# Sliding-window attention beside an SSM convolution: one DRAM tensor for Z and u·D, and loads of 96 rows in place of 32

## The chip, the cores and the metric

The kernel runs on one core of one Trainium2 chip. The core has a matrix engine (PE, with a separate row PEld for its weight loads), a vector engine (DVE), a scalar engine (ACT), GpSimd (POOL) and SyncE (SP). SP and POOL issue the transfers (DMAs) here; sixteen DMA engines move the data. Every engine works through its own instructions in order, and semaphores tie the engines together. The metric is device time in microseconds; each kernel is run several times and the median is given.

## The reference

Two independent halves are computed and put side by side, each 2048 positions by 640 channels:

- *Half a*: `qkv = x @ wqkv`, 32 heads of 20; each position attends to the 8 positions `s, s-2, ..., s-14` (those before the start are masked); softmax over the 8; weighted sum of `v`; then `@ wo`.
- *Half b*: for each channel `d` a convolution of `u` with a kernel `K[d, l] = Re(sum_n C[d,n] exp(dt[d] A[d,n] l) dt[d] B[d,n])`, with 192 states `n`, done in the reference through an FFT of twice the length (`y = irfft(rfft(u) * rfft(K))[:2048]`, rounded to bf16), and then `y + u * Dskip`.

Inputs and outputs are bf16.

## The kernel before

**Channels and chunks.** The 640 channels of half b are worked on in five chunks of 128 (`NCH = 5`). For one chunk the kernel first builds the convolution kernel `K` from tables (`trig_half`, `small_half`, `y_form`, `kgen_unit`), then transforms `K` and `u` (`fwd`), multiplies the spectra (`products`) and does the first half of the inverse transform (`inverse_a`). The result is `Z`, a tile of 128 partitions by 4096: 32 frequencies times 4 channel groups on the partitions (frequency major, group minor), and along the row the real part of 64 positions times 32 channels followed by the imaginary part.

**What goes through DRAM.** Three scratch tensors carry data from the chunks to later work. `Sd` holds the spectrum of `u`: it is stored by `fwd_u` (L394) and loaded back by `products` as `P1` (L353) and, with its halves exchanged, as `P2` (L354, L355); the two products with the spectrum of `K` are L357. `Zd` holds `Z`, stored by `inverse_a` (L376) as soon as its fourth piece is done. `UDd` holds `u * Dskip`: `times_d` multiplies half a chunk at a time on DVE (L386) into one buffer `UD` of 128 partitions by 1024, and SP stores it (L387), ten times in all. In `UD` the partition is group major, position minor, the other way round from `Z`.

**The end of half b.** `Inverse` finishes the inverse transform. Its 64 positions are cut into four quarters of 16; for one quarter the tile `self.t[qr]` has 96 partitions: 32 rows for the real part, 32 for the imaginary part, 32 for `u * Dskip`. The constant `HB` on the same 96 partitions holds cosines, sines and an identity, so one matmul (L676) does the second transform step and adds `u * Dskip`. `Inverse.load` fills a quarter chunk by chunk, three transfers of 32 rows for each chunk (L664), 60 transfers in all; in the first and fourth quarter they alternate between SP and POOL, in the others all are on SP. A row has four pieces (one per channel group) of 512 elements. `Inverse.part` does two or three positions: matmuls into `ps_ib`, an ACT copy into `ysb` (L677), and after every eighth position four stores of 32 partitions to the output (L680) on SP. `ysb` has four such groups, used in turn.

**The order of the work.** The chunks' loop in `body` issues the stages of half b, then attention starts: projections of `k`, `q` and `v`, products of `q` and `k` on DVE (L529, L532), logits on PE (L543), softmax, and the weighted sum `av_step` (products on DVE at L603, summed on PE into `ps_o`), with the output projection `out_piece` (`ps_op`, stores at L637). The parts of `Inverse` are dealt out between the steps of `av_step` by the lists `inside` and `behind`; quarter 0 and 1 are loaded before that loop, quarters 2 and 3 chunk by chunk from within it (`LOADS`). A quarter's tile takes the place of an older tile: quarter 1 that of `kT` (last read by the products of L532), quarter 2 that of `prod`, quarter 3 that of `xT` (last read by the projection of `v`), and its loads wait until these have been read.

Where a call is not marked with `keep_in_program_order`, a scheduler in the framework puts the instructions of each engine in order by its own estimates; from `att.in_order()` on, PE, ACT and the softmax keep the order written. The DMAs of SP stand in the order that this scheduler chose. Each DMA from SP counts up one of eight semaphores in turn, so that the ninth waits for the first.

Between the last `times_d` and the P1 load of chunk 3, `load_x` has SP issue four transposing loads of `x` into `xT` (L431).

Of the kernel before, what the change touches and what calls it, by code (L numbers as in the profile page):

```python
# [13 lines left out]
bf16 = mybir.dt.bfloat16  # L14
f32 = mybir.dt.float32

NCH = 5
# [64 lines left out]
def inline(nc, arr, name):  # L82
    return nc.inline_tensor(np.ascontiguousarray(arr).astype(np.float32).astype(ml_dtypes.bfloat16), name=name).ap()


def partB_prep(tc, pools, prm):
# [33 lines left out]
    for nm in ("B_B_re", "B_B_im", "B_C_re", "B_C_im"):  # L120
        load(nm)
# [144 lines left out]
def bc(ap, axis, n):  # L266
    s = list(ap.shape)
    return ap.unsqueeze(axis).to_broadcast(s[:axis] + [n] + s[axis:])
# [94 lines left out]
def inverse_a(tc, pools, C, P1, P2, Zd, pool):  # L363

    nc = tc.nc
    MM = nc.tensor.matmul
    Z = pool.tile([128, 128, 32], bf16, name="Z", tag="sp", bufs=3)

    def piece(b):
        ps = pools["psum"].tile([128, 8, 128], f32, name="ps_ia", tag="bank2")  # L370
        for j in range(8):
            for w, P in enumerate((P1, P2)):
                MM(ps[:, j], lhsT=P[:, 8 * b + j].rearrange("p k g -> p (k g)"), rhs=C["EA"][:, w, :], start=(j % 4 == 0 and w == 0), stop=(w == 1), skip_group_check=True)  # L373
        nc.scalar.copy(out=Z[:, :, 8 * b:8 * b + 8], in_=ps[:].rearrange("p j x -> p x j"))  # L374
        if b == 3:
            nc.sync.dma_start(out=Zd, in_=Z[:].rearrange("p x j -> p (x j)"))  # L376

    return [lambda b=b: piece(b) for b in range(4)]


def times_d(tc, pools, C, UDd, c, i):

    nc = tc.nc
    U = C["U"][:].rearrange("p l (ut c) -> p c l ut", c=NCH)[:, c]
    UD = pools["tabb"].tile([128, 32, 32], bf16, name="UD", tag="UD")
    tc.keep_in_program_order(nc.vector.tensor_tensor(out=UD[:], in0=U[:, 32 * i:32 * i + 32], in1=bc(C["Dsb"][:, c], 1, 32), op=A.mult))  # L386
    nc.sync.dma_start(out=UDd[c, :, 1024 * i:1024 * i + 1024], in_=UD[:].rearrange("p l j -> p (l j)"))  # L387


def fwd_u(tc, pools, C, Sd, c):  # L390
# [11 lines left out]
class Attention:  # L402
# [4 lines left out]
    def __init__(self, tc, pools, A_x, A_wqkv, A_wo, out_a, psk, psg):  # L407
        self.tc, self.nc, self.ta, self.ident = tc, tc.nc, pools["bbase"], pools["ident"]
        self.A_x, self.A_wo, self.out_a = A_x, A_wo, out_a
        self.wsrc = A_wqkv.rearrange("(kt k) c -> k kt c", k=128)  # L410
        self.big = lambda name: psk.tile([128, 2, 512], f32, name=name, tag="bank2")
        self.one = lambda name: psg.tile([128, 512], f32, name=name, tag="bank", bufs=2)
        self.lsb, self.at, self.obs = {}, {}, {}
        self.nav = self.nob = 0
        self.MM = self.nc.tensor.matmul
        self.SC = self.VV = lambda ins: ins
# [226 lines left out]
class Inverse:  # L643


    def __init__(self, att, a2, Zd, UDd, out_b):
        self.att, self.nc, self.a2, self.Zd, self.UDd = att, att.nc, a2, Zd, UDd
        self.dst = out_b.rearrange("(l1 l0) (g ch) -> g l1 l0 ch", l0=64, g=4)
        self.HB = att.ta.tile([96, 64, 32], bf16, name="HB", tag="TA1")
        self.nc.gpsimd.dma_start(out=self.HB[:].rearrange("p a n -> p (a n)"), in_=inline(self.nc, fft_consts_np()["HB"], "c_HB"))  # L650
        self.t = {}
# [4 lines left out]
    def load(self, qr, c0=0, c1=NCH):  # L656
        nc = self.nc
        pool, tag = ((self.a2, "Z"), (self.att.ta, "LPC"), (self.att.a1, "prod"), (self.att.ta, "U"))[qr]
        if c0 == 0:
            self.t[qr] = pool.tile([96, 4, NCH, 16, 32], bf16, name="Z", tag=tag)  # L660
        for c in range(c0, c1):
            for ri in range(3):
                src = self.UDd[c, :, 512 * qr:512 * qr + 512] if ri == 2 else self.Zd[c, :, 2048 * ri + 512 * qr:2048 * ri + 512 * qr + 512]
                (nc.sync, nc.gpsimd)[(c + ri) % 2 if qr in (0, 3) else 0].dma_start(out=self.t[qr][32 * ri:32 * ri + 32, :, c].rearrange("p g l n -> p g (l n)"), in_=src.rearrange("(g p) n -> p g n" if ri == 2 else "(p g) n -> p g n", g=4))  # L664

    def part(self, l0, n):
        nc = self.nc
# [15 lines left out]
        return [(lambda l0=8 * q + l, n=n: self.part(l0, n)) for q in range(8) for l, n in ((0, 3), (3, 3), (6, 2))]  # L683


def body(tc, ctx, pools, prm, B_u, B_Dskip, Sd, Zd, UDd, A_x, A_wqkv, A_wo, out_a, out_b):
    nc = tc.nc
    cn = fft_consts_np()
    bbase = ctx.enter_context(tc.tile_pool(name="taba", bufs=1, reuse_waits="tile"))
# [9 lines left out]
    C = dict(BD=BD, T2=T2, EA=EA, Dsb=Dsb, U=U)  # L699
# [25 lines left out]
    att = Attention(tc, pools, A_x, A_wqkv, A_wo, out_a, psk, psg)  # L725
# [5 lines left out]
    def unit(c, h, uu, F, G, X, between=lambda: None):  # L731
        Ys = [y_form(tc, pools, F, G, uu, k) for k in range(3)]
        between()
        kgen_unit(tc, dict(pools, psum=psg), 2 * h + uu, X, Ys, Kb[c])
        if 4 * c + 2 * h + uu in UD_AFTER:
            times_d(tc, pools, C, UDd, *divmod(UD_AFTER.index(4 * c + 2 * h + uu), 2))

    def q_first():
        att.open_first(pools["tabb"])
# [5 lines left out]
    UD_AFTER = [2, 3, 5, 6, 7, 9, 10, 11, 13, 14]  # L745
# [75 lines left out]
            att.products(1, w, ct, ct + 1)  # L821
    fft.close()
    a2 = ctx.enter_context(tc.tile_pool(name="a2", bufs=1, side="right", reuse_waits="tile"))
    inv = Inverse(att, a2, Zd, UDd, out_b)
    inv.load(0)
    att.open_v()
    for w in range(W):
# [35 lines left out]
    for i0, ni, j0, nj, done, inside, behind in (  # L863
# [7 lines left out]
        for w in range(W):  # L871
# [5 lines left out]
            if (done, w) in LOADS:  # L877
                qr, c = LOADS[done, w]
# [9 lines left out]
@with_exitstack  # L888
def kernel(
    ctx: ExitStack,  # L890
    tc: tile.TileContext,
    A_x: bass.AP,
    A_wqkv: bass.AP,
    A_wo: bass.AP,
    B_u: bass.AP,
    B_A_re: bass.AP,
    B_A_im: bass.AP,
    B_B_re: bass.AP,
    B_B_im: bass.AP,
    B_C_re: bass.AP,  # L900
    B_C_im: bass.AP,
    B_log_dt: bass.AP,
    B_Dskip: bass.AP,
    out: bass.AP,
):
    nc = tc.nc
    prm = dict(B_A_re=B_A_re, B_A_im=B_A_im, B_B_re=B_B_re, B_B_im=B_B_im, B_C_re=B_C_re, B_C_im=B_C_im, B_log_dt=B_log_dt)
    out_a = out[0][:, 0:640]
    out_b = out[0][:, 640:1280]
    pools = {}  # L910
    pools["const"] = ctx.enter_context(tc.tile_pool(name="const", bufs=1))
    idc = nc.inline_tensor(np.eye(128, dtype=np.float32).astype(ml_dtypes.bfloat16), name="ident_c")
    ident = pools["const"].tile([128, 128], bf16, name="ident")
    nc.sync.dma_start(out=ident[:], in_=idc.ap())
    pools["ident"] = ident
    dpool = ctx.enter_context(tc.tile_pool(name="dram", bufs=1, space=bass.MemoryType.DRAM))
    Sd = dpool.tile([NCH, 128, 4096], bf16, name="Sdram")
    Zd = dpool.tile([NCH, 128, 4096], bf16, name="Zdram")
    UDd = dpool.tile([NCH, 128, 2048], bf16, name="UDdram")
    body(tc, ctx, pools, prm, B_u, B_Dskip, Sd, Zd, UDd, A_x, A_wqkv, A_wo, out_a, out_b)  # L920


# [28 lines left out]
```

## Time and profile before

| | us |
|---|---|
| median of 3 runs | 422.47 (420.15 to 423.2) |
| the profiled execution | 420.89 |
| its span | 419.0 |
| busy: PE / DVE / ACT / POOL | 343.7 / 380.0 / 310.4 / 44.6 |
| SP, all issues of the 10 stores of UD | about 0.32 each |
| SP, issue of one load of 32 rows of Z | about 0.59 |

Moved in all: 51.57 MB, 123 GB/s on average; 41.40 MB of it on SP's queue. The share of busy time is an average over stages with different limits. The views that are quoted below give start and duration in microseconds; in brackets stands how long an engine had been idle before an instruction and what released it. A line such as L664 is a line of the kernel as printed above, SPq is SP's instruction queue, and "issue" in the chain of work is time in which an engine waited for nothing that the profile shows.

### The profile page before, as it was taken

To read this page: it belongs to the slowest core of one execution; us is meant where nothing else is said; L and a number is where in the kernel's file an instruction comes from. 1 tells how busy PE (TensorE), PEld (TensorE's weight loads), DVE (VectorE), ACT (ScalarE), POOL (GpSimd) and SP (SyncE) were. 2 spreads that over 40 slices of the span, in tenths; PEclk is the share of its full clock that TensorE was granted. 3 is DMA by queue.
4 is the path that set the end of the run, shared out by engine and by line. 5 is a ranking of instruction groups with operands and counts; after the bars stand their busy time and mean duration, and the time that the engine had idled before them with its cause. 6 is when DMAs were issued, how large, how long until landed. Compare 5 with 4: busy or idle time off the path is not lost.

```text
span 419.0 us, 17077 instructions
## 1 busy us (share of the span) xinstructions
PE 343.7 (82%) x7757; PEld 232.6 (56%) x7757; DVE 380.0 (91%) x353; ACT 310.4 (74%) x571; POOL 44.6 (11%) x85
## 2 busy tenths in 40 slices
PE   2476679968888787786967798999899999789896
PEld 1133575845855577554755567455455676445454
DVE  7999999799997999999999989984986999999842
ACT  3988988789899899969999682533667644745652
POOL 7520000000000000000010000040000300502110
PEclk9997889999898899989989988999999999969889
DMA  5599003261333313344029990610040382887643
GB/s 144 182 226 162 3 2 127 89 214 34 127 128 129 85 22 127 127 130 102 15 115 304 188 250 9 242 78 2 3 102 0 109 183 86 222 233 206 186 122 108
DMA packets 45129, 51.57 MB, mean 123 GB/s; under 512 B 31376, under 2 KB 38992, under 8 KB 42368
## 3 DMA queue, kind: packets, MB, share of 16 engines
q1 hardware_dynamic: 41520, 41.40, 36.2%
q0 software_dynamic: 3392, 8.95, 7.0%
q8 instruction: 61, 1.00, 1.0%
q10 hardware_dynamic: 144, 0.12, 0.1%
q14 instruction: 12, 0.10, 0.1%
HBM read 28.01 MB, written 18.35 MB: 111 GB/s over the span
## 4 chain that ended last, share of the span: by engine, by line
PE 40%; ACT 23%; DVE 21%; issue 9%; DMA 4%; SPq 3%; DVEq 0%; ACTq 0%
PE ps_k L322 8%; ACT R L223 6%; ACT A L337 6%; ACT Sg L343 5%; PE ps_q L490 4%; PE ps_k L472 4%; PE ps_v L503 4%; PE ps_op L421 4%; DVE Y L307 3%; DMA P<-Sdram 3%; DVE X L277 3%; ACT Z L374 3%; PE ps_ph L248 2%; PE ps_l L543 2%; PE ps_ph L252 2%
## 5 line engine op out<-in xcount | busy, mean ns | idle before, releaser
L307 DVE TENSOR_TENSOR Y<-F,G 128x3072 bf16<-128x3072 bf16 x60 | 103.0, 1758 | 2.5 <-PE ps_k L322 2.5
L322 PE MATMUL ps_k<-Y,X 64*32 64x64 bf16 (+1 forms) x3840 | 80.8, 237 | 17.3 <-issue 7.8
L322 PEld LDWEIGHTS <-X 64*32 64x32 bf16 (+1 forms) x3840 | 61.8, 115 | 44.3 <-issue 28.4
L223 ACT ACTIVATE R<-LPC 128x192 bf16<-128x192 f32 x225 | 59.5, 358 | 0.1
L248 PE MATMUL ps_ph<-LPC 128*128 128x512 bf16 x100 | 33.1, 434 | 11.9 <-DMA LPC<-lo 5.9
L343 ACT CAST Sg<-ps_f 128x1024 bf16<-128x1024 f32 x40 | 37.6, 1027 | 5.8 <-PE ps_f L342 5.8
L342 PE MATMUL ps_f<-A,T 128*128 128x128 bf16 x320 | 26.3, 252 | 17.2 <-ACT A L337 16.2
L337 ACT CAST A<-ps_f 128x1024 bf16<-128x1024 f32 x40 | 38.0, 1042 | 2.1 <-PE ps_f L336 2.0
L342 PEld LDWEIGHTS <-T 128*128 128x128 bf16 x320 | 24.6, 115 | 18.6 <-issue 17.6
L277 DVE TENSOR_TENSOR X<-R,TX 128x3072 bf16<-128x3072 bf16 x20 | 34.3, 1758 | 0.0
L260 ACT ACTIVATE TA<-ps_ph 128x1024 bf16<-128x1024 int16 (+1 forms) x40 | 30.5, 831 | 4.4 <-PE ps_ph L252 2.4
L603 DVE TENSOR_TENSOR prod<-v,atp 128x2048 bf16<-128x2048 bf16 (+2 forms) x32 | 30.9, 1016 | 2.2 <-PE ps_o L421 1.3
L260 ACT ACTIVATE TX<-ps_ph 128x1024 bf16<-128x1024 int16 (+1 forms) x40 | 30.0, 843 | 1.7 <-PE ps_ph L252 1.4
L532 DVE TENSOR_TENSOR prod<-qT,kT 128x1024 bf16<-128x1024 bf16 (+1 forms) x16 | 23.0, 1481 | 4.7 <-ACT qT L491 4.7
L357 DVE TENSOR_TENSOR P<-P,Sg 128x4096 bf16<-128x4096 bf16 x10 | 22.9, 2289 | 3.4 <-DMA P<-Sdram 1.7
L421 PE MATMUL ps_op<-wo,o 128*128 128x320 bf16 x160 | 25.0, 304 | 0.4 <-DVE recip L572 0.3
L373 PE MATMUL ps_ia<-EA,P 128*128 128x128 bf16 x320 | 23.2, 231 | 0.9 <-DVE P L357 0.9
L374 ACT CAST Z<-ps_ia 128x1024 bf16<-128x1024 f32 x20 | 19.5, 1014 | 5.9 <-PE ps_ia L373 4.7
L336 PE MATMUL ps_f<-BD,U 128*64 128x128 bf16 x320 | 20.2, 283 | 4.2 <-ACT Z L374 3.5
L635 ACT CAST ob<-ps_op 128x320 bf16<-128x320 f32 x28 | 11.8, 431 | 15.0 <-PE ps_op L421 12.5
L490 PE MATMUL ps_q<-xT,wkq 128*128 128x512 bf16 x100 | 22.6, 379 | 0.0
L472 PE MATMUL ps_k<-xT,wkq 128*128 128x512 bf16 x100 | 22.4, 379 | 0.0
(132 smaller groups left out, 591.1 us busy)
## 6 DMA issues: line engine op xcount, KB each, us to landing
Sdram<-Sg SPq DMA_DIRECT2D x5, 1024.0 KB
P<-Sdram SPq DMA_DIRECT2D x5, 1024.0 KB
P<-Sdram SPq DMA_DIRECT2D x10, 512.0 KB
Zdram<-Z SPq DMA_DIRECT2D x5, 1024.0 KB
Z<-Zdram SPq DMA_DIRECT2D x30, 128.0 KB
U<-in_B_u_dram SPq DMA_DIRECT2D x4, 640.0 KB
UDdram<-UD SPq DMA_DIRECT2D x10, 256.0 KB
out_dram<-ysb SPq DMA_DIRECT2D x32, 80.0 KB
```

What stands on the lines that cost most here:

```text
L223: last = nc.scalar.activation(out=R[:, :, e, :], in_=src, func=ACT.Exp, scale=m)
L248: MM(full[:, 16 * gi:16 * gi + 16], lhsT=L[b][:, 0:128], rhs=C, start=(i == 0), stop=(i == len(ops) - 1))
L260: last = nc.scalar.activation(out=dst[:, q0:q0 + nq, 0:32, :].rearrange("p q e f -> p e q f"), in_=words.rearrange("p (e q f) -> p e q f", ...
L277: TT = lambda o, a, b, op: V.tensor_tensor(out=o, in0=a, in1=b, op=op)
L307: nc.vector.tensor_tensor(out=Y[:].rearrange("p q (b a) f -> p q b a f", a=8), in0=fa, in1=gb, op=A.mult)
L322: MM(ps[32 * g:32 * g + 32, t], lhsT=X[hb, q, 2 - k, :, f], rhs=Ys[k][hb, q, :, f], start=(t == 0 and n == 0), stop=(n == 5), tile_positio ...
L337: nc.scalar.copy(out=A1[:, :, 32 * b:32 * b + 32].rearrange("p k (j g) -> p k j g", g=4), in_=ps[:].rearrange("p j k g -> p k j g"))
L342: last = MM(ps[:, kk], lhsT=C["T2"][:, 8 * b + kk, :], rhs=A1[:, 8 * b + kk, :], start=(kk % 4 == 0), stop=True, skip_group_check=True)
L343: nc.scalar.copy(out=Sg[:, :, 8 * b:8 * b + 8, :], in_=ps[:].rearrange("p k (j g) -> p j k g", g=4))
L421: self.MM = lambda *a, **k: late(self.nc.tensor.matmul(*a, **k))
L472: MM(ps[:, i], lhsT=self.wk[:, kt, 128 * ct:128 * ct + 128], rhs=self.x4[:, kt, 2 * i:2 * i + 2, 256 * hf:256 * hf + 256], start=(kt == 0) ...
L490: MM(ps[:, i], lhsT=self.wq[:, kt, 128 * ct:128 * ct + 128], rhs=self.x4[:, kt, 2 * i:2 * i + 2, 256 * hf:256 * hf + 256], start=(kt == 0) ...
```

## The change

`Zd` becomes one tensor of shape `[5, 3, 128, 2048]`: real part, imaginary part and `u * Dskip`, each 128 rows of 2048. The store of `Z` writes the two parts of a row to two places. `times_d` writes its rows in the same order as `Z` (frequency or position major, group minor); as its tile is group major, the store becomes four, one for each group of 32 partitions. With that the three parts of a quarter are evenly spaced rows, and one transfer of 96 rows by four pieces replaces three of 32; all of them are issued by SP, none by POOL.

```diff
-            nc.sync.dma_start(out=Zd, in_=Z[:].rearrange("p x j -> p (x j)"))
+            nc.sync.dma_start(out=Zd[0:2].rearrange("r p n -> p r n"), in_=Z[:].rearrange("p (r l) j -> p r (l j)", r=2))
...
-def times_d(tc, pools, C, UDd, c, i):
+def times_d(tc, pools, C, Zd, c, i):
...
-    nc.sync.dma_start(out=UDd[c, :, 1024 * i:1024 * i + 1024], in_=UD[:].rearrange("p l j -> p (l j)"))
+    dst = Zd[2].rearrange("(p g) n -> g p n", g=4)[:, :, 1024 * i:1024 * i + 1024]
+    for g in range(4):
+        nc.sync.dma_start(out=dst[g], in_=UD[32 * g:32 * g + 32].rearrange("p l j -> p (l j)"))
...
-            for ri in range(3):
-                src = self.UDd[c, :, 512 * qr:512 * qr + 512] if ri == 2 else self.Zd[c, :, 2048 * ri + 512 * qr:2048 * ri + 512 * qr + 512]
-                (nc.sync, nc.gpsimd)[(c + ri) % 2 if qr in (0, 3) else 0].dma_start(out=self.t[qr][32 * ri:32 * ri + 32, :, c].rearrange("p g l n -> p g (l n)"), in_=src.rearrange("(g p) n -> p g n" if ri == 2 else "(p g) n -> p g n", g=4))
+            src = self.Zd[c].rearrange("r (p g) n -> (r p) g n", g=4)[:, :, 512 * qr:512 * qr + 512]
+            nc.sync.dma_start(out=self.t[qr][:, :, c].rearrange("p g l n -> p g (l n)"), in_=src)
...
-            times_d(tc, pools, C, UDd, *divmod(UD_AFTER.index(4 * c + 2 * h + uu), 2))
+            k, i = divmod(UD_AFTER.index(4 * c + 2 * h + uu), 2)
+            times_d(tc, pools, C, Zd[k], k, i)
...
-    Zd = dpool.tile([NCH, 128, 4096], bf16, name="Zdram")
-    UDd = dpool.tile([NCH, 128, 2048], bf16, name="UDdram")
+    Zd = dpool.tile([NCH, 3, 128, 2048], bf16, name="Zdram")
```

More of the change, by code (lines that the diff above doesn't have):

```diff
@@ L643, with __init__ @@
 class Inverse:
-    def __init__(self, att, a2, Zd, UDd, out_b):
-        self.att, self.nc, self.a2, self.Zd, self.UDd = att, att.nc, a2, Zd, UDd
+    def __init__(self, att, a2, Zd, out_b):
+        self.att, self.nc, self.a2, self.Zd = att, att.nc, a2, Zd
         self.dst = out_b.rearrange("(l1 l0) (g ch) -> g l1 l0 ch", l0=64, g=4)
@@ L683, in parts, with body @@
         return [(lambda l0=8 * q + l, n=n: self.part(l0, n)) for q in range(8) for l, n in ((0, 3), (3, 3), (6, 2))]
-def body(tc, ctx, pools, prm, B_u, B_Dskip, Sd, Zd, UDd, A_x, A_wqkv, A_wo, out_a, out_b):
+def body(tc, ctx, pools, prm, B_u, B_Dskip, Sd, Zd, A_x, A_wqkv, A_wo, out_a, out_b):
     nc = tc.nc
@@ L823, in body @@
     a2 = ctx.enter_context(tc.tile_pool(name="a2", bufs=1, side="right", reuse_waits="tile"))
-    inv = Inverse(att, a2, Zd, UDd, out_b)
+    inv = Inverse(att, a2, Zd, out_b)
     inv.load(0)
@@ L917 @@
     Sd = dpool.tile([NCH, 128, 4096], bf16, name="Sdram")
[L918 to L920 removed]
+    Zd = dpool.tile([NCH, 3, 128, 2048], bf16, name="Zdram")
+    body(tc, ctx, pools, prm, B_u, B_Dskip, Sd, Zd, A_x, A_wqkv, A_wo, out_a, out_b)
 _INS = ['A_x', 'A_wqkv', 'A_wo', 'B_u', 'B_A_re', 'B_A_im', 'B_B_re', 'B_B_im', 'B_C_re', 'B_C_im', 'B_log_dt', 'B_Dskip']
```

## The prediction

> **What bounds the kernel now.** I read the page first. One execution spans 419.0 us (420.89 us with what lies around the span), DVE is busy for 91% of it and PE for 82%, while the row of DMA busy tenths has zeros beside nines.
>
> ```profile
> span 419.0 us, 17077 instructions
> ...
> PE 343.7 (82%) x7757; PEld 232.6 (56%) x7757; DVE 380.0 (91%) x353; ACT 310.4 (74%) x571; POOL 44.6 (11%) x85
> ...
> DMA  5599003261333313344029990610040382887643
> ```
>
> The reader is to see that no share of the whole decides anything here: the change touches DMAs alone, so it counts only where a transfer ends a wait. For that I read the chain of work that ended last (columns: start us, us, what), from its end backwards.
>
> ```profile
> 381.93 1.85 SPq L680
> 383.78 0.04 issue
> ...
> 390.30 3.12 DMA Z<-Zdram
> ...
> 393.44 0.60 PE ps_ib L421 x24
> ...
> 415.52 0.49 DVE ob L633
> ```
>
> The last 25.6 us are PE work without a gap (393.44 to the DVE cast at 415.52 and the store behind it), and ahead of them the chain runs for some twelve us through SP's queue: output stores (L680), 0.04 us between one issue and the next, then loads of Z for the third and fourth quarter (L664), and 3.12 us in which the last of them lands. The PE timeline (idle time before, and its releaser, in brackets) gives the size of that wait, and DVE's shows who else stands still.
>
> ```profile
> 366.61 0.75 PE L421 MATMUL ps_ib<-Z,HB 96*32 96x160 bf16 x24
> ...
> 391.05 0.66 PE L421 MATMUL ps_o<-prod,ident 32*32 32x256 bf16 x40
> 393.44 0.60 PE L421 MATMUL ps_ib<-Z,HB 96*32 96x160 bf16 x24 [1.74 <-DMA Z<-Zdram]
> ```
>
> ```profile
> 391.42 2.43 DVE L603 TENSOR_TENSOR prod<-v,atp 128x1024 bf16<-128x1024 bf16 x3 [0.74 <-PE ps_o L421]
> 394.41 1.23 DVE L603 TENSOR_TENSOR prod<-v,atp 128x2048 bf16<-128x2048 bf16 x1 [0.56 <-PE ps_o L421]
> ```
>
> PE sat for 1.74 us because the third quarter's tile was not there; DVE waited in that stretch for PE (0.74 and 0.56 us), not the other way round. So 1.74 us is what an earlier landing is worth here. The wait falls where it does because SP works in order, and the loads are interleaved with stores that wait for ACT. Sizes of both, from SP's timeline of the last third:
>
> ```profile
> 349.79 1.19 SPq L664 DMA_DIRECT2D Z<-Zdram  x2
> ...
> 360.06 1.23 SPq L664 DMA_DIRECT2D Z<-Zdram  x1
> 365.33 2.61 SPq L680 DMA_DIRECT2D out_dram<-ysb  x4
> ```
>
> Between the load that was issued at 360.06 and the first store at 365.33 SP only waited.
>
> There is a second place where a transfer is on the chain, 150 us earlier: the product of chunk 3's spectra (P, L357).
>
> ```profile
> 241.13 3.76 ACT Sg L343 x4
> ...
> 247.04 0.68 ACT TA L260
> 247.72 0.86 issue
> 248.59 2.29 DVE P L357
> 250.88 1.68 DVE Y L307
> ...
> 252.60 0.48 PE ps_k L322 x20
> ```
>
> Sg, which this product also reads, left ACT at 241.13 + 3.76 = 244.89. The view names ACT's TA as releaser, but L260 writes nothing that P reads, and 0.86 us of "issue" lie between the two, where a hand-over elsewhere takes 0.04 (the row at 383.78 is one). What else P needs is the load of P1 from Sdram, so I take that load to have landed at about 248.5. SP's timeline shows why it came late.
>
> ```profile
> 225.79 0.32 SPq L387 DMA_DIRECT2D UDdram<-UD  x1
> 226.21 15.30 SPq L431 DMA_TRANSPOSE xT<-in_A_x_dram  x4
> 241.61 0.52 SPq L353 DMA_DIRECT2D P<-Sdram  x1
> 243.66 0.46 SPq L354 DMA_DIRECT2D P<-Sdram  x1
> ```
>
> P1's load at 241.61 stood behind four transposing loads of x (15.30 us of issue), and these behind the UD store of 225.79. Whatever lengthens that store moves the transposes, P1's load, the product at 248.59, the Y behind it and PE's matmuls at 252.60, all on the chain.
>
> **The change part by part.** The order of instructions in the built program says what moves: the orders of PE, ACT and DVE stay as they are; POOL loses its 14 loads of Z; SP issues 20 loads of 96 rows for 46 of 32, and 40 UD stores of 32 rows for 10 of 128; and all 20 loads now stand in SP's queue ahead of all 32 output stores of ysb. Three durations are needed (min/median/max in ns of an issue on SP):
>
> ```profile
> L387 SPq DMA_DIRECT2D UDdram<-UD x10: 319/322/351, 68.8 to 225.8; - x10
> ```
>
> ```profile
> L680 SPq DMA_DIRECT2D out_dram<-ysb x32: 315/464/1849, 365.3 to 407.8; - x32
> ```
>
> ```profile
> L664 SPq DMA_DIRECT2D Z<-Zdram x30: 542/594/1478, 332.3 to 390.3; - x30
> ```
>
> 1. *The loads of the last two quarters.* SP alone, issuing a 128 KB load every 0.6 us, kept the DMA engines at a share of 0.57 and 169 GB/s; with POOL and the stores beside it the share was 0.95 at 239 GB/s (windows from 349.80 and 365.00; the last three columns are the clock granted to PE, DMA share and GB/s).
>
> ```profile
> core 0: us, PE busy (x) PEld busy (x) DVE busy (x) ACT busy (x) POOL busy (x), PEclk, DMA share, GB/s
> 349.80:362.00 12.20, 11.15 (x288) 6.61 (x281) 11.28 (x12) 6.83 (x10) 2.13 (x4) 1.00 0.57 169
> 365.00:375.00 10.00, 8.40 (x220) 4.02 (x220) 10.00 (x11) 5.93 (x12) 1.21 (x3) 0.66 0.95 239
> 395.00:410.00 15.00, 14.91 (x316) 8.04 (x316) 8.67 (x8) 9.76 (x21) 1.62 (x3) 0.80 0.49 123
> ```
>
> The ten loads of 384 KB for the last two quarters are 3.93 MB: at 169 to 239 GB/s that is 16.4 to 23.3 us from the gate at about 360.1 (xT's last reader and PE's first free moment for the third quarter), so they have landed by 377 to 384, and PE asks for the third quarter at 391.05 + 0.66 = 391.71. The wait of 1.74 us goes. What is late next? PE's own work, 14.91 of the 15 us from 395; DVE runs at PE's pace there. Bounds: 0, if the loads still come late, and 1.74; I take −1.74. The issue time of a 96-row transfer is in no row. From below it is a 32-row issue, 0.59; from above three of them, 1.8. Even at 1.8 us the ten are issued by 378.5, so both ends give −1.74. The second quarter, gated at 349.79, is five loads: 1.97 MB, 11.6 us at 169 GB/s, landed by 361.4, before the first matmul on it in the row at 366.61. Stores now queue behind the loads, but the ring of ysb holds four groups and its first slot is written again only after 391.71. At nothing, then, with PE's other work as cover; without that cover one more load time, about 3.1 us.
>
> The Trainium skill, "DMA: Bandwidth & Descriptors", section "Issuing engines are not separate DMA queues", says that issuing from several engines only saves the sequencer's time, which is usually small beside the transfer. Here the trace disagrees: at 0.57 the engines waited for SP. By the page the merged loads would gain nothing from fewer issues; the sum does not need that gain, only the place in the queue.
>
> 2. *The UD stores.* One issue of 0.32 us becomes four. Nearest row: a 32-row store of ysb, median 0.46, min 0.315, max 1.85. With 0.04 us between issues four take 4 × 0.46 + 3 × 0.04 = 1.96, so what follows on SP is 1.64 us later; 1.06 us with the minimum. At nine of the ten places something covers it: behind the second store of the two pairs stands a P1 load, as in chunk 2, where the pair below ends at 175.03 + 6.54 = 181.57 and the product that reads P1 starts sixteen us later; behind the others stand stores of Sg and Z, or nothing.
>
> ```profile
> 175.03 6.54 SPq L387 DMA_DIRECT2D UDdram<-UD  x2
> ```
>
> ```profile
> 197.28 2.30 DVE L357 TENSOR_TENSOR P<-P,Sg 128x4096 bf16<-128x4096 bf16 x1
> ```
>
> At 225.79 nothing covers it. Part may be taken back by the first transpose, which alone took longer than its sisters:
>
> ```profile
> 226.21 4.46 SPq L431 DMA_TRANSPOSE xT<-in_A_x_dram  x1
> ```
>
> 4.46 against (15.30 − 4.46) / 3 = 3.61: 0 to 0.85 us, since it shared the engines with a 1 MB store; I take 0.4. So +1.24 us (bounds 0, if P1's load was not the releaser after all, and 1.64). The second half of P2 waits until 243.66 anyway, and P1 at 242.85 is still ahead of it.
>
> 3. *One buffer for UD.* The next UD product must wait until all four pieces have landed. The tightest pair is the one above: SP issues from 175.03, DVE writes again at 179.90.
>
> ```profile
> 179.90 1.32 DVE L386 TENSOR_TENSOR UD<-U,Dsb 128x1024 bf16<-128x1024 bf16 x1
> ```
>
> Three pieces later is 175.03 + 1.5 = 176.53; a 160 KB store of the same kind lands 2.0/3.5/5.0 us after its issue:
>
> ```profile
> DMA to landing us min/median/max: 2.0/3.5/5.0
> ```
>
> That is 178.5, 180.0 or 181.5 for 179.90: 0, 0.1 or 1.6 us, and DVE is not on the chain there. I take 0.
>
> 4. *Z stored in rows of 4 KB instead of 8 KB, and POOL without loads.* The last of the five stores is read back by the first quarter's loads, which SP has issued before the second quarter's gate at 349.79 and PE wants only shortly before the row at 366.61; the earlier four have whole chunks of time. POOL has no work that waits behind its loads but the output stores. 0 for both.
>
> Sum: −1.74 + 1.24 = −0.5 us on 420.89, that is 420.4. The profiled execution stands 1.6 us below the median of the three runs (422.47; 420.15 to 423.2); on the median's footing the forecast is 422.0 us. One per cent is 4.2 us, about what a measurement of this kernel can tell from no change, so this is "same".
>
> **The rivals.**
>
> A. *Only the gain.* The transposes absorb the delay, or P1's load was not what P waited for: −1.74, 420.7. For it: the profile does name ACT as the releaser. Against: the 0.86 us without a cause.
>
> B. *The pieces hold SP for longer (slower).* With t us for each piece, SP reaches the transposes 4t − 0.2 us later, and with 0.4 taken back and 1.74 gained the net is 4t − 2.34: it turns to a loss at t = 0.59, and passes 1% at t = 1.64. At 1.85, the longest store of ysb, it is +5.1 us, 427.6. For it: issues next to a busy DMA did get that long, and the store at 225.79 meets a 1 MB store. Against: the single issue at that very spot took 0.32. The Trainium skill, "DMA: Bandwidth & Descriptors", section "Anatomy of one DMA", gives a DMA a fixed cost of about 2.0 us; paid one after another by four pieces that would be some +5.7 us by the same formula, an estimate. Loads 0.6 us apart show that here such costs overlap, so this gets a small chance.
>
> C. *Merging does not cheapen the issue.* The dearest issue of many small rows is this one:
>
> ```profile
> L720 SPq DMA_DIRECT2D U<-in_B_u_dram x4: 597/1182/2988, 23.4 to 31.9; - x4
> ```
>
> At 2.99 us each the second quarter lands at 349.8 + 15 + 3.1 = 367.9, 1.3 us late for 366.61, and the ten others at about 393.5, so that the old wait stays: 1.24 + 1.3 = +2.5, 425.0.
>
> D. *The clock.* In 395 to 410 PE was granted 0.80 and was busy throughout. Without the pause it may get full speed there, 3 us more: −3.5, 419.0. Nothing shows that the pause caused the low clock.
>
> **How the numbers follow.** The rivals' times stand on the 420.89 of the profiled execution. Forecast 0.48 (its own range 420.9 to 422.4: −1.74 + 1.06 − 0.85 to −1.74 + 1.64), A 0.18, B 0.20 (half of it past 1%), C 0.07, D 0.07. Faster by over 1% needs D and A together (−4.7): 0.05. Slower: 0.10 from B and 0.02 from C, where a late second quarter would also hold DVE. Within 1%: 0.83. The range takes in D at 419.0 with the spread of the runs, and reaches into B: 418.5 to 426.
>
> **What would show it.** In the changed profile: no wait of PE's ps_ib for Z near 391; twenty Z loads ahead of the first ysb store on SP, landed before 385; four UD issues at about 225.8 that total near 2 us, the transposes starting near 227.8, and P (L357) near 249.8 instead of 248.59, with the Y and ps_k behind it as much later. The forecast is wrong if a UD piece takes more than 0.6 us, if a 96-row issue takes more than 1.8 us, or if P stays at 248.6.

## The result: slower by 1.4%, and the profile after

The changed kernel takes 427.52 us (median of six runs, 425.62 to 429.91) against 421.34 us for the kernel before (six runs, 419.22 to 423.2): a ratio of 1.014, 95% interval 1.0093 to 1.0187. The forecast was 422.0 us, range 418.5 to 426; the time lies outside it. The profiled execution of the changed kernel took 425.62 us, its span is 423.8 us, 4.8 us more than before. Here and below a ratio goes by the executions that were not in a slower state, a median by all of them, so a ratio can differ by some half a per cent from the quotient of two medians.

From the page of the changed kernel, the head, the PE row and the DMA row of the 40 slices, and the two queues that carry instructions (packets, MB, share of 16 engines):

```profile
span 423.8 us, 17050 instructions
...
PE 336.1 (79%) x7739; PEld 227.9 (54%) x7757; DVE 380.7 (90%) x353; ACT 310.6 (73%) x571; POOL 38.9 (9%) x71
...
DMA  5599003262334403334149971700040658994153
...
q8 instruction: 60, 0.98, 1.0%
...
q14 instruction: 12, 0.10, 0.1%
```

The busy times are no higher than they were (DVE 380.7 for 380.0, PE lower); the time that was added is idle time. At 360 us the two profiles are still close together: the first exponentials of the attention start 0.3 us later. ACT's timeline, before and then after:

```profile
360.09 1.91 ACT L562 ACTIVATE lsb<-lsb 128x2048 bf16<-128x2048 bf16 x1
```

```profile
360.39 1.91 ACT L564 ACTIVATE lsb<-lsb 128x2048 bf16<-128x2048 bf16 x1
```

The loss lies between 363 and 386 us. The chain of work that ended last, after, in that stretch (start us, us, what):

```profile
363.35 0.47 PE ps_ib L423 x14
363.82 2.71 issue
366.52 0.45 PE ps_ib L423 x6
...
370.57 0.44 PE ps_o L423 x5
371.00 4.11 issue
375.12 0.85 PE ps_o L423 x23
...
380.64 0.28 PE ps_o L423 x5
380.92 0.94 issue
381.86 0.37 PE ps_o L423 x11
```

Three times PE stops and the profile shows nothing that it waits for: 2.71 + 4.11 + 0.94 = 7.76 us. Each time it stops in the middle of a group: 14 of 20 matmuls of `ps_ib`, then the pause, then the other 6; 5 of 16 of `ps_o`, then 11. The matmuls on both sides of such a pause read the same tiles. Before, there is one pause of that kind in the stretch, 0.94 us (PE's timeline, before; the later rows are for the sum below):

```profile
368.73 0.54 PE L421 MATMUL ps_o<-atp,ident 32*32 32x384 bf16 x14 [0.94 <-issue]
...
370.78 1.89 PE L421 MATMUL ps_s<-lsb,ident 128*128 128x256 bf16 x8
...
375.24 0.84 PE L421 MATMUL ps_op<-wo,o 128*128 128x320 bf16 x5 [0.30 <-DVE recip L572]
...
376.32 0.85 PE L421 MATMUL ps_op<-wo,o 128*128 128x320 bf16 x5
...
377.41 1.53 PE L421 MATMUL ps_op<-wo,o 128*128 128x320 bf16 x10
...
407.96 7.46 PE L421 MATMUL ps_op<-wo,o 128*128 128x320 bf16 x50
```

The same matmuls in PE's timeline after:

```profile
369.57 0.99 PE L423 MATMUL ps_ib<-Z,HB 96*32 96x160 bf16 x24
...
377.17 1.89 PE L423 MATMUL ps_s<-lsb,ident 128*128 128x256 bf16 x8
...
382.16 1.38 PE L423 MATMUL ps_op<-wo,o 128*128 128x320 bf16 x5
...
383.95 1.51 PE L423 MATMUL ps_op<-wo,o 128*128 128x320 bf16 x5
...
385.84 1.53 PE L423 MATMUL ps_op<-wo,o 128*128 128x320 bf16 x10
...
399.48 0.66 PE L423 MATMUL ps_o<-prod,ident 32*32 32x256 bf16 x40
400.36 0.72 PE L423 MATMUL ps_ib<-Z,HB 96*32 96x160 bf16 x24 [0.23 <-ACT ob L637]
...
413.06 7.46 PE L423 MATMUL ps_op<-wo,o 128*128 128x320 bf16 x50
```

Laid side by side, the lateness grows and then shrinks: `ps_ib` x24 366.61 to 369.57 (+2.96), `ps_s` 370.78 to 377.17 (+6.39), the first `ps_op` x10 377.41 to 385.84 (+8.43), the third quarter's `ps_ib` x24 393.44 to 400.36 (+6.92), the last `ps_op` x50 407.96 to 413.06 (+5.10). The sum of the parts:

| part | us |
|---|---|
| late from the head | +0.30 |
| pauses of PE without a releaser, 7.76 − 0.94 | +6.82 |
| the two `ps_op` x5 behind them, 1.38 + 1.51 for 0.84 + 0.85 (granted clock 0.53 for 1.00) | +1.20 |
| the wait for Z, 1.74 before, 0.23 (for ACT) now | −1.51 |
| from the third quarter's `ps_ib` to the last `ps_op` | −1.82 |
| rest (the difference; slower matmuls against shorter waits for ACT) | +0.11 |
| sum | +5.10 |

The +1.20 need not come from the pauses: in experiment 1 below, whose only pause there is 0.19 us, the same matmuls took 1.49 + 1.33 us at a granted clock of 0.54.

Before the change DVE worked through this stretch almost without a pause (10.00 of the ten us from 371, in the table below), so PE had time to spare there, as experiment 8 shows. Now DVE waited for PE behind the longest pause (DVE's timeline, after):

```profile
375.73 0.96 DVE L605 TENSOR_TENSOR atp<-v,atp 128x1536 bf16<-128x1536 bf16 x1 [3.80 <-PE ps_o L423]
```

What else differs in that stretch is the load on the DMA engines. Busy time by window, the last three columns being granted PE clock, DMA share and GB/s (the share adds up the times of all packets over sixteen engines, so it can pass 1); before, then after:

```profile
350.00:361.00 11.00, 10.37 (x272) 6.21 (x264) 10.90 (x12) 5.83 (x9) 1.13 (x2) 1.00 0.56 168
361.00:371.00 10.00, 7.41 (x270) 3.71 (x255) 9.05 (x12) 7.62 (x15) 5.00 (x10) 0.80 1.02 254
371.00:381.00 10.00, 9.53 (x190) 5.09 (x192) 10.00 (x10) 4.59 (x10) 1.13 (x2) 0.86 0.70 192
381.00:391.00 10.00, 10.00 (x202) 5.45 (x178) 9.69 (x12) 6.24 (x13) 2.70 (x5) 1.00 0.78 238
```

```profile
350.00:361.00 11.00, 10.37 (x264) 6.21 (x256) 10.85 (x12) 5.52 (x9) 0.82 (x2) 1.00 0.93 231
361.00:371.00 10.00, 6.66 (x223) 3.22 (x205) 8.42 (x11) 6.81 (x12) 1.49 (x3) 0.71 1.08 251
371.00:381.00 10.00, 5.59 (x131) 2.69 (x128) 5.53 (x7) 3.47 (x7) 0.00 (x0) 0.60 1.12 236
381.00:391.00 10.00, 9.14 (x139) 4.57 (x138) 9.36 (x9) 3.89 (x9) 1.67 (x3) 0.83 0.43 107
```

Before, the engines are full for some ten us at a time. After, the merged loads keep them full from 350 to 381 us (0.93, 1.08, 1.12), and the three pauses lie in that stretch and at its end.

**A first reading.** The two instruction queues moved 0.98 + 0.10 MB for 17050 instructions, 63 bytes each; a q8 packet is 0.98 MB / 60 = 16.3 KB, so 258 instructions. A matmul is two of them (PE and its weight load): 129 matmuls. Counted in PE's timeline, the first and second pause are 127 matmuls apart, the second and third 128. So PE stops at the ends of such blocks. **Theory F** is that the instructions themselves come late, because the packet that brings them competes with full DMA engines. The Trainium skill, "Runtime: NRT & Kernel Launch", section "Instruction fetch mechanics", says that instructions are refilled in 16 KiB blocks of 256 by a DMA queue of the sequencer, and that crossing a block's end is "mostly hidden". The trace agrees on the block; it disagrees on hidden: 4.11 us for one.

### The profile page after: what moved, and what is told of

Its sections match the earlier page's. It is cut to its first block, busy times and chain, and to the rows that moved or that the text cites. A ratio compares the mean times of both kernels' runs of the same rounds, so it can differ in the third digit from the quotient of the medians.

```text
span 423.8 us, 17050 instructions
## 1 busy us (share of the span) xinstructions
PE 336.1 (79%) x7739; PEld 227.9 (54%) x7757; DVE 380.7 (90%) x353; ACT 310.6 (73%) x571; POOL 38.9 (9%) x71
## 4 chain that ended last, share of the span: by engine, by line
PE 41%; ACT 22%; DVE 20%; issue 10%; DMA 5%; SPq 1%; DVEq 0%; ACTq 0%
PE ps_k L322 7%; ACT R L223 6%; PE ps_op L423 6%; ACT A L337 5%; PE ps_q L492 4%; PE ps_k L474 4%; DVE Y L307 4%; PE ps_v L505 4%; DMA P<-Sdram 4%; DVE X L277 4%; ACT Sg L343 4%; PE ps_o L423 3%; ACT Z L374 2%; PE ps_l L545 2%; PE ps_ib L423 2%
## 5 line engine op out<-in xcount | busy, mean ns | idle before, releaser
L248 PE MATMUL ps_ph<-LPC 128*128 128x512 bf16 x82 | 28.2, 429 | 14.4 <-DMA LPC<-lo 6.2
L342 PE MATMUL ps_f<-A,T 128*128 128x128 bf16 x320 | 22.5, 228 | 17.7 <-ACT A L337 15.9
L342 PEld LDWEIGHTS <-T 128*128 128x128 bf16 x320 | 20.5, 102 | 19.5 <-issue 18.5
L373 PE MATMUL ps_ia<-EA,P 128*128 128x128 bf16 x320 | 22.3, 225 | 2.6 <-DVE P L357 2.6
L323 ACT CAST Ksb<-ps_k 128x512 bf16<-128x512 f32 x20 | 11.6, 595 | 16.8 <-PE ps_k L322 16.8
L252 PE MATMUL ps_ph<-LPC 128*64 128x256 bf16 x200 | 20.3, 303 | 2.8 <-ACT Sg L343 1.6
```

Of the source, the lines that this page charges most:

```text
L248: MM(full[:, 16 * gi:16 * gi + 16], lhsT=L[b][:, 0:128], rhs=C, start=(i == 0), stop=(i == len(ops) - 1))
L342: last = MM(ps[:, kk], lhsT=C["T2"][:, 8 * b + kk, :], rhs=A1[:, 8 * b + kk, :], start=(kk % 4 == 0), stop=True, skip_group_check=True)
```

## The experiments

All kernels keep the orders of PE, ACT and DVE of the changed kernel, but for what an edit adds (and, in 6, two neighbouring weight loads that change places); a ratio is to the kernel before, run beside it. The letters are explained in the expectations. The edits are cut to their main lines: in 1, 6, 7 and 9 the loads of quarters 2 and 3 from within the loop (`LOADS`) go as well, and in these four and in 8 SP's stores of `ysb` are held in program order.

**1. The three loads of 32 rows again, ahead of the stores.** The changed kernel, with its one tensor and its four u·D pieces:

```diff
-            nc.sync.dma_start(out=self.t[qr][:, :, c].rearrange("p g l n -> p g (l n)"), in_=src)
+            for ri in range(3):
+                self.att.tc.keep_in_program_order(nc.sync.dma_start(out=self.t[qr][32 * ri:32 * ri + 32, :, c].rearrange("p g l n -> p g (l n)"), in_=src[32 * ri:32 * ri + 32]))
...
+        if done == 0:
+            inv.load(2)
+            inv.load(3)
```

> The changed kernel with every load of 96 rows put back into three of 32 rows, all on SP, and all still ahead of the stores of ysb. Theory F (fetch): the loads of 384 KB filled the DMA engines without a pause from 352 to 380 us, and the transfers that bring PE's instructions came late behind them; PE stood still for 2.71, 4.11 and 0.94 us with nothing to wait for. Three loads of 128 KB take SP three issues of 0.6 us, some 205 GB/s, so the engines keep room: gaps of PE under 1 us each between 360 and 385, no wait of ps_ib for Z near 391, and a time of 419 to 421.5 us. Rival S (stores): it is the place of the stores behind the loads that costs; order unchanged, so 426 to 428. Rival W (wait): PE's gaps are waits for a transfer that the profile does not name; same loads in the same order, so 2 to 4 us gaps stay.

417.80 us against 419.73; ratio 0.9961 (0.9928 to 0.9994): faster than both, and below the 419 to 421.5 that F forecast. The interval ends just below 1. PE's timeline has the pause at 0.19 us and no wait for Z; the window shows why the engines had air:

```profile
368.23 0.54 PE L423 MATMUL ps_o<-atp,ident 32*32 32x384 bf16 x12 [0.19 <-issue]
...
392.85 0.72 PE L423 MATMUL ps_ib<-Z,HB 96*32 96x160 bf16 x24 [0.23 <-DMA out_dram<-ysb]
```

```profile
350.00:361.00 11.00, 10.36 (x276) 6.20 (x269) 10.69 (x12) 6.22 (x9) 1.52 (x3) 1.00 0.56 177
```

SP needs three issues for one, and the share falls from 0.93 to 0.56. Everything else of the change is still in this kernel, so the loss comes with the merged loads. F's mechanism held, and the two other theories named there (S and W) did not.

**2. The merged loads without the u·D pieces.** One store of 128 rows per half chunk. This kernel leaves out the reordering of u·D, which then lies in other rows than the loads expect.

```diff
-    for g in range(4):
-        nc.sync.dma_start(out=dst[g], in_=UD[32 * g:32 * g + 32].rearrange("p l j -> p (l j)"))
+    nc.sync.dma_start(out=Zd[2][:, 1024 * i:1024 * i + 1024], in_=UD[:].rearrange("p l j -> p (l j)"))
```

> The changed kernel with the UD store as one transfer of 128 rows again. It leaves out the reordering of u times D: these rows are stored in their own order, so u times D is added at the wrong positions; sizes and places of all transfers are as in the changed kernel otherwise. Theory F: the cost is in the merged loads, so 425.5 to 428 us, with PE's gaps of 2 to 4 us between 360 and 385. Rival U (the UD pieces and what they delay): back to 420 to 422.

425.74 us, ratio 1.0119 (1.0077 to 1.0161). The pauses stand at the same matmuls (2.36, 3.84 and 0.75 us):

```profile
373.59 0.53 PE L421 MATMUL ps_o<-atp,ident 32*32 32x384 bf16 x11 [3.84 <-issue]
```

Nearly the whole loss is there without the pieces; U fell.

**3. The pieces alone.** The kernel before with its u·D store in four.

```diff
-    nc.sync.dma_start(out=UDd[c, :, 1024 * i:1024 * i + 1024], in_=UD[:].rearrange("p l j -> p (l j)"))
+    for g in range(4):
+        nc.sync.dma_start(out=UDd[c, 32 * g:32 * g + 32, 1024 * i:1024 * i + 1024], in_=UD[32 * g:32 * g + 32].rearrange("p l j -> p (l j)"))
```

> The kernel before with only the UD store cut into four transfers of 32 rows. Theory F: the pieces delay the transposes by about 1.4 us and P (L357) of chunk 3 by about 0.9 us, of which 0.3 us is left at 360 us: 421 to 422.5 us, within 0.3% of before. Rival U: 426 to 428.

420.65 us, ratio 1.0012 (0.997 to 1.0053): no loss that can be told from none.

**4. The same work with the block ends elsewhere.** The changed kernel with 32 small extra matmuls in `sums(0)`, ahead of this stretch, whose result is overwritten; every later matmul stands 32 places further on in the stream of instructions, so a block ends 32 matmuls earlier in the work.

```diff
+        for n in range(32 if hf == 0 else 0):
+            self.MM(self.ps_s[:, 0:8], lhsT=self.ident[:], rhs=self.lsb[hf][:, 0, 0:8], start=True, stop=True)
```

> The changed kernel with 32 small matmuls (64 instructions with their weight loads) added in front of the first sums (near 325 us); they write what the sums then overwrite. Theory F: PE stops where a block of instructions ends, every 128 matmuls, so each gap moves 32 matmuls forward in the order: the one behind the 14th ps_ib of its group to behind the 6th of the 24 ps_o ahead of that group, the one behind 5 of 16 ps_o to behind the 29th of the 32 ps_o ahead of the 24 ps_ib. Gaps together 5 to 9 us, still 128 matmuls apart. Rival W: a wait belongs to an instruction, so the gaps stay in front of the same ps_ib and ps_o.

A single run: 422.14 us, span 420.4. PE's timeline:

```profile
361.54 0.40 PE L423 MATMUL ps_o<-atp,ident 32*32 32x512 bf16 x6
363.48 0.42 PE L423 MATMUL ps_o<-atp,ident 32*32 32x512 bf16 x10 [1.55 <-issue]
...
371.87 0.50 PE L423 MATMUL ps_o<-atp,ident 32*32 32x384 bf16 x2 [3.95 <-issue]
...
379.37 0.50 PE L423 MATMUL ps_o<-prod,ident 32*32 32x384 bf16 x19 [0.87 <-issue]
```

The first pause stands 10 + 8 + 14 = 32 matmuls earlier, moved from the fifteenth `ps_ib` of a group to the seventh `ps_o` of an earlier one, and the next two follow at 128 and 127, with 6.37 us in all. A wait for data or for a buffer would have stayed with its matmul (W fell). With the packets shown below, this settles that PE waits for instructions; what makes them late is the matter of the other runs.

**5. Half the size, the same rate.** Two transfers of 192 KB for one of 384 KB.

```diff
-            nc.sync.dma_start(out=self.t[qr][:, :, c].rearrange("p g l n -> p g (l n)"), in_=src)
+            for k in (0, 2):
+                nc.sync.dma_start(out=self.t[qr][:, k:k + 2, c].rearrange("p g l n -> p g (l n)"), in_=src[:, k:k + 2])
```

> The changed kernel with each load cut into two of 96 rows by two pieces (192 KB), in the same place in SP's order. SP can still issue them faster than the DMA engines move them (192 KB in 0.6 us is 320 GB/s against the 250 seen). Eight may be under way at a time, 1.57 MB instead of 3.15. Theory D (depth: what delays the instructions is the amount queued ahead): about 6 us queued instead of 12, so PE's gaps at the block ends shrink to under 2 us each, sum 1 to 3.5 us instead of 7.8, and 421 to 424 us. Theory A (busy engines are enough): gaps as in the changed kernel, 2 to 4 us, 425 to 428.

420.03 us, ratio 1.0035 (0.9985 to 1.0084). The engines were as full (0.93, 1.07, 0.91 in the three windows from 350) and moved more, 266 GB/s in the first. But only one pause is left:

```profile
370.33 0.53 PE L423 MATMUL ps_o<-atp,ident 32*32 32x384 bf16 x11 [1.86 <-issue]
```

By the share alone all three pauses should have stayed, so it does not set their size by itself (A fell; D's 1 to 3.5 us of pauses held, though the time lies below its 421).

**6. Loads of 384 KB, paced.** Two tiny transfers behind each load hold SP back (`late` is `keep_in_program_order`); the loads still stand ahead of the stores.

```diff
+            for k in range(2):
+                n = self.n_small = self.n_small + 1
+                late(nc.sync.dma_start(out=self.small[:, 8 * n - 8:8 * n], in_=self.small_src[16 * (n % 8):16 * (n % 8) + 16, 0:8]))
```

> The changed kernel with two small transfers (16 rows of 16 bytes) behind each load of 384 KB, all loads ahead of the stores. The eight turns then hold at most three loads, about 1.15 MB, while the issue of a load with its small ones takes some 1.4 us for 384 KB, still above 250 GB/s. Theory D: gaps as with half, sum under 3 us, 420 to 423 us. Theory Z (what counts is the length of one transfer's run on each DMA engine, 24 pieces of 1 KB): gaps stay 2 to 4 us, 425 to 428. Theory A: the same as Z.

419.02 us, ratio 0.9995 (0.9946 to 1.0044). The same 384 KB transfers, at a share of 0.68 in the first window, cost nothing that can be measured; one pause of 2.57 us is left. It is not the shape of the merged load that hurts (Z and A fell; D's pauses held, its 420 to 423 us did not).

**7. Loads of 32 rows, unpaced.** Experiment 1 with its loads dealt between SP and POOL, so that they are issued as fast as the merged ones.

```diff
-                self.att.tc.keep_in_program_order(nc.sync.dma_start(out=self.t[qr][32 * ri:32 * ri + 32, :, c].rearrange("p g l n -> p g (l n)"), in_=src[32 * ri:32 * ri + 32]))
+                self.att.tc.keep_in_program_order((nc.sync, nc.gpsimd)[(c + ri) % 2 if qr else 0].dma_start(out=self.t[qr][32 * ri:32 * ri + 32, :, c].rearrange("p g l n -> p g (l n)"), in_=src[32 * ri:32 * ri + 32]))
```

> Loads of 32 rows again, ahead of the stores, but for the second to the fourth quarter dealt out between SP and POOL, so that the DMA engines are kept as busy as in the changed kernel (share 0.95 or more from 351 to 372). Theory A: gaps of 2 to 4 us, 424 to 428 us. Theory D: at most eight loads of 128 KB from SP and a few from POOL are queued, about 1.5 MB, gaps 0 to 2 us each, 418 to 422. Theory Z: eight pieces per engine in one transfer, no gaps over 1 us, 418 to 420.

425.89 us, ratio 1.0169 (1.0092 to 1.0247). Shares 0.93, 1.08 and 1.06, three pauses of together 5.36 us, the longest:

```profile
371.64 0.54 PE L423 MATMUL ps_o<-atp,ident 32*32 32x384 bf16 x14 [3.21 <-issue]
```

The old 32-row loads lose about as much as the merged ones once they come fast enough (four executions alone stand behind this ratio). D's forecast was too low and Z's fell. A's held here, but A had been wrong for the half-sized loads.

**8. Merged loads in the old order.** 384 KB, interleaved with the output stores as before the change.

```diff
-            nc.sync.dma_start(out=self.t[qr][:, :, c].rearrange("p g l n -> p g (l n)"), in_=src)
+            ins = nc.sync.dma_start(out=self.t[qr][:, :, c].rearrange("p g l n -> p g (l n)"), in_=src)
+            if qr > 1:
+                self.att.tc.keep_in_program_order(ins)
```

> The changed kernel with the loads of quarters 2 and 3 and the stores of ysb held in the order in which the program states them, which is the order of SP in the kernel before: ten loads, then stores and loads in turn. All loads are still of 384 KB. Theory D: the stores hold the later loads back, the queue never holds more than the second quarter's five, so at most one gap of 1 to 2 us near 363, and the wait of ps_ib for Z near 391 is back with 0 to 2 us: 420.5 to 423.5. Theory Z: gaps stay where loads run, 424 to 428.

420.18 us, ratio 1.0019 (0.9972 to 1.0066). The stores between the loads give the engines pauses (0.72 and 0.71 in the first two windows). There is no pause near 363 us and no wait for Z, both against D; one pause of PE, 0.88 us, stands at 390.84. Instead PE, at a granted clock of 1.00 in the first two windows, came early to the output projection and waited there for DVE:

```profile
375.02 1.49 PE L423 MATMUL ps_op<-wo,o 128*128 128x320 bf16 x5 [3.57 <-DVE recip L574]
```

So PE had up to 3.6 us to spare against DVE in this stretch. The window from 371 with its share of 1.02 tests little here: PE used only 76 matmuls in it, fewer than a block holds.

**9. The order alone.** The kernel before, all Z loads on SP, 32 rows each, ahead of the stores.

```diff
-                (nc.sync, nc.gpsimd)[(c + ri) % 2 if qr in (0, 3) else 0].dma_start(out=self.t[qr][32 * ri:32 * ri + 32, :, c].rearrange("p g l n -> p g (l n)"), in_=src.rearrange("(g p) n -> p g n" if ri == 2 else "(p g) n -> p g n", g=4))
+                self.att.tc.keep_in_program_order(nc.sync.dma_start(out=self.t[qr][32 * ri:32 * ri + 32, :, c].rearrange("p g l n -> p g (l n)"), in_=src.rearrange("(g p) n -> p g n" if ri == 2 else "(p g) n -> p g n", g=4)))
...
+        if done == 0:
+            inv.load(2)
+            inv.load(3)
```

> The kernel before with one edit: the loads of the four quarters are all issued by SyncE, 32 rows each as before, ahead of the stores of the quarters; layout, tensors and the single u-D store are those before. Theory F (the loss of the change is matmul instructions that come late while the DMA engines are kept full; the gain is loads that are issued ahead of the stores): SyncE issues a 32-row load in about 0.6 us, so the engines have pauses as in the run with three loads of 32 rows, the wait of the matmuls for Z near 391 us is gone (-1.7 us), no gap of TensorE without a releaser above 1 us between 360 and 391 us, and without the four u-D pieces another -0.9 near 250 us: ratio 0.990 to 0.997, at or below that of the run with three loads (0.996). Rival (the gain of that run came from the one tensor with one row order, whose rows a load reads as 4 KB): ratio 0.998 to 1.004 here.

417.53 us against 419.97, ratio 0.9961 (0.9923 to 0.9999): the ratio of experiment 1 without the new tensor, and again only just clear of none. So the gain needs neither the new layout nor larger loads; it comes with all loads on SP ahead of the stores. This edit also takes the 14 loads from POOL, and no run parts the two, though the 1.74 us wait for Z that the place should remove is gone. That no pause above 1 us would be seen was wrong:

```profile
368.16 0.37 PE L421 MATMUL ps_o<-atp,ident 32*32 32x384 bf16 x12 [2.85 <-issue]
```

Together (share by the window views, pauses of PE without a releaser from 360 to 391 us):

| kernel | share 350–361 / 361–371 / 371–381 | pauses, us | ratio |
|---|---|---|---|
| before | 0.56 / 1.02 / 0.70 | 0.94 | 1 |
| after | 0.93 / 1.08 / 1.12 | 7.76 | 1.014 |
| 1 three loads, first | 0.56 / 1.02 / 0.61 | 0.19 | 0.9961 |
| 2 merged, one UD store | 1.03 / 1.09 / 1.05 | 6.95 | 1.0119 |
| 3 UD in four | 0.69 / 0.94 / 0.74 | 0.89 | 1.0012 |
| 4 shifted | 1.03 / 1.08 / 1.02 | 6.37 | – |
| 5 half | 0.93 / 1.07 / 0.91 | 1.86 | 1.0035 |
| 6 paced | 0.68 / 1.03 / 0.71 | 2.57 | 0.9995 |
| 7 32 rows, SP and POOL | 0.93 / 1.08 / 1.06 | 5.36 | 1.0169 |
| 8 merged, old order | 0.72 / 0.71 / 1.02 | 0.88 | 1.0019 |
| 9 order alone | 0.70 / 0.98 / 0.63 | 2.85 | 0.9961 |

Every kernel with more than 5 us of pauses had a share above 0.9 in all three windows and above 1.0 in the last; all with a share below 0.75 in the first window stayed under 3 us. The half-sized loads are the odd one out. A single pause under 3 us does not show in the ratio (6 and 9). In 9 DVE was busy for 10.00 and 9.53 us of the two windows from 361 in spite of the pause. In the four kernels with more than 5 us of pauses DVE was busy for only 5.5 to 7.9 us of the ten from 371, in all others for 9.3 or more. So a pause seems to cost time once DVE runs out of work; no run tried that by itself.

**The instruction packets themselves.** The traces also hold every single DMA packet, though no view prints them one by one. Each packet of q8 has 16,384 bytes. At 64 bytes an instruction (16,384 over the 256 of 128 matmuls and their weight loads), 60 of them are 15,360 instructions, nearly all of PE's 15,514 (7757 matmuls and as many weight loads). After the change such packets start at 363.77, 372.24, 379.31 and 383.35 us and take 1.2 to 1.5 us each; the three pauses end at 366.52, 375.12 and 381.86, each time 1.3 to 1.7 us after a packet's end. The eleven kernels together have 27 pauses of PE of more than 0.11 us without a releaser between 340 and 420 us, and each of the 27 ends 1.0 to 1.7 us after the end of a packet of q8. That is what PE waited for.

The packet itself is not slower with full engines: 1.2 us, where it took 0.9 to 1.4 us from 353 to 389 before the change. It starts late. Behind the first two pauses the next packet starts 5.72 and 4.19 us after PE has gone on, behind the third 1.49 us, where the share has fallen to 0.43. Behind the longest pause of experiment 7 it is 5.75 us, with the half-sized loads of experiment 5 it is 2.4. After the change PE used the 127 matmuls between the first two pauses in 371.00 − 366.52 = 4.48 us, while the packets started 372.24 − 363.77 = 8.47 us apart. This fits one block that is fetched ahead while PE works on another; the request itself is in no row.

**What stays open** is why the start of a packet is late by so different amounts among the full kernels: how much is queued ahead of it, or how many queues it shares the engines with.

## Why the prediction was wrong

*What bounds the kernel.* For the last 25 us the reading was right: PE and what it waits for set them. From 365 to 375 the prediction's own window row has DVE busy for 10.00 of 10 us, so there DVE, not PE, set the pace. What was not read either is the row of 0.94 us of "issue" at 368.73, in a window whose share was quoted (0.95); it stood in the very view from which the wait for Z was taken.

*Step 1, the loads of the last two quarters: the gain came, and the step failed.* SP's timeline after:

```profile
225.70 1.72 SPq L389 DMA_DIRECT2D Zdram<-UD  x4
227.52 15.00 SPq L433 DMA_TRANSPOSE xT<-in_A_x_dram  x4
242.56 0.58 SPq L353 DMA_DIRECT2D P<-Sdram  x1
...
332.47 38.03 SPq L665 DMA_DIRECT2D Z<-Zdram  x20
370.59 42.85 SPq L681 DMA_DIRECT2D out_dram<-ysb  x32
```

The issues on SP of the pieces of u·D and of the loads, after (min/median/max in ns):

```profile
L389 SPq DMA_DIRECT2D Zdram<-UD x40: 302/420/1528, 69.1 to 227.0; - x40
```

```profile
L665 SPq DMA_DIRECT2D Z<-Zdram x20: 544/722/3127, 332.5 to 367.4; - x20
```

Twenty loads ahead of the first store, all issued by 370.5; the third quarter's `ps_ib` at 400.36 waits for nothing of Z. The row −1.51 of the sum is this gain, for −1.74 forecast. A 96-row issue took 0.72 us by the median, between the bounds 0.59 and 1.8 (three of the 20 took 2.51 to 3.13). The rate, 231 to 251 GB/s in the windows from 350 to 381, was at the upper end of the range of 169 to 239 and above it. The step that failed is the sentence "What is late next? PE's own work": I asked what the next wait for *data* would be, and gave the faster stream a gain (0 to 1.74) and no price. Its price is the missing term: +6.82 us in which PE waits for its own instructions. Experiment 4 and the packets of q8 show that it is instructions; experiments 1, 6 and 7 show that it comes with loads that keep the engines full, with experiment 5 as the exception. The term was put at nothing without a reason, and the bounds of the step should have reached above zero for it.

*The citation in step 1.* That SP alone left the engines idle (0.57) was right. The sentence that the sum did not need the faster issue missed that the faster issue could harm: experiments 1 and 9 take the same place in the queue with slow issues and gain 0.4%, and experiment 7, with two engines issuing, loses.

*Step 2, the UD pieces: mechanism right, size smaller.* Four issues took 1.72 us (1.96 forecast), the transposes started at 227.52, P1's load at 242.56 is 0.95 later than before, and the product too:

```profile
249.50 2.29 DVE L357 TENSOR_TENSOR P<-P,Sg 128x4096 bf16<-128x4096 bf16 x1 [2.66 <-DMA P<-Sdram]
```

249.50 for a forecast of 249.8, and the releaser is now named: the load, as taken from the 0.86 us without a cause. But of the 0.91 us only 0.30 are left at 360 us; carrying +1.24 to the end was too much by about 0.9. Experiment 3 agrees: 1.0012.

*Steps 3 and 4* cost nothing that a row shows.

*The rivals.* Their times do not stand on 420.89, as the prediction says, but on the median: 422.47 − 1.74 = 420.7, and so on for the others. C's 393.5 does not come out of its own rate either: fifteen issues of 2.99 us from 349.8 and 3.1 us behind them give 397.8. A's mechanism is not what happened, though experiments 1 and 9 gain about its 0.4%. B got the sign right for the wrong reason: a piece took 0.42 us by the median, under its point of decision of 0.59 (four of the 40 took 0.82 to 1.53, none of them at 225.70), and experiment 2 keeps the loss without the pieces. The section of the Trainium skill that B cites ("DMA: Bandwidth & Descriptors", "Anatomy of one DMA") is about transfers issued by GpSimd, while SP issues the pieces; the four issues at 225.70 took 1.72 us in all. C fell (0.72 us an issue). D has something in it: behind the old wait PE was granted 0.56 (393.44 to 400.00) and after the change 1.00 (400.36 to 405.00), and that stretch is 1.82 us shorter; but the clock was lower around the pauses (0.71 and 0.60 for 0.80 and 0.86). The 0.12 for "slower" was all on B and C. No rival has the mechanism that cost the time, so the chance given to "slower" was no foresight.

*The signs.* Two of the three signs of being wrong came up, a piece above 0.6 us and a 96-row issue above 1.8, and neither is what cost the time.

## What to carry to other kernels

Idle time of PE that begins inside a group of equal matmuls and is put down to "issue" is a sign of late instructions; count the matmuls from one such pause to the next (here 127 and 128), and shift the stream by a few matmuls to prove it. Before transfers are made faster or moved together, ask what else uses the DMA engines. Where the matmuls are short (127 of them in 4.48 us here) and the engines stay full for tens of us, the instructions can come too late; smaller or paced transfers avoided most of it here. And separate the place of a transfer in its queue from its size: here all loads on SP ahead of the stores were worth 0.4%, just clear of noise, and the rate of the merged loads took back some 1.8% (1.014 against 0.9961).

## What the runs showed of the hardware

- PE's instructions come in packets of 16,384 bytes, and PE stopped every 127 or 128 matmuls where they came late. With the engines full from 350 to 381 us a block's end cost PE up to 4.11 us, and three in a row 7.76 us. The packet took 1.2 us all the same; its start was late, 5.72 and 4.19 us after PE had gone on for 1.49 with the engines half idle.
- 32-row loads from two queues starve PE like 96-row loads from one (5.36 us of pauses); half-sized loads at nearly the same share do so much less (1.86 us).
- The issue of a transfer took SP 0.72 us by the median for 96 rows by four pieces, and 0.59 us for 32 rows.
- The granted clock changes within a few us. The ten matmuls of 128x320 behind the pauses took 1.38 + 1.51 us at 0.53, where the kernel before took 0.84 + 0.85 at 1.00; experiment 1, with hardly a pause, took 1.49 + 1.33 at 0.54, so no pause is needed for it. Later matmuls of the changed kernel ran at 1.00 where the kernel before had 0.56. No run tried what sets it.
